# A feed-forward product with 20 small products for two halves of D, four chunks of F and three blocks of tokens, in place of Strassen's seven

## The chip, the cores and the metric

The kernel runs on one NeuronCore of a Trainium2 chip. TensorE (PE in the profile) multiplies matrices, VectorE (DVE) and ScalarE (ACT) work on SBUF and PSUM, GpSimd (POOL) works on SBUF alone, SyncE (SP) issues most of the DMAs. The metric is the device time of one execution in microseconds. The kernel before takes 1905.74 us, the median of three runs (1905.74 to 1906.42).

## The reference

```python
# x: (8, 3008, 256); w_in: (256, 2048); w_out: (2048, 256), all float32
X = np.fft.fft(np.fft.fft(x, axis=1), axis=2).real      # per batch: a 2-D DFT, real part
t = X.reshape(8 * 3008, 256)
h = t @ w_in
g = np.maximum(h, 0.0) ** 2
out = g @ w_out                                         # (24064, 256)
```

## The kernel before, in words

**Fronts.** For a batch b the DFT over the sequence is made as two tables, Pt and Qt (128 rows by NKT = 1505 frequencies), and one row that every partition needs, Et (spread over 128 partitions). The DFT over D is folded into w_in once, as G1, G2 and the column gE. Frequencies k and S-k share their work: with hP = G1'Pt and hQ = G2'Qt, the hidden rows are hP + gE Et + hQ for k and hP + gE Et - hQ for the mirrored frequency. The frequencies go in blocks of CK = 256 (the last has 225); a block is n columns of k and n of the mirrored ones, so 2n tokens. For each block a loop runs over NJ = 8 steps j; a step handles the chunks j and j + 8 of the 16 chunks of 128 of F. `front` (L887) does the four products of a step (L896) into two PSUM banks, hP and hQ, each 2 chunks by n; VectorE makes t = hP + gE Et (L900, twice) and then g = t + hQ (L903) and t - hQ reversed (L904). `relu` (L909) and `square` (L912) run in place on ScalarE. A front bank comes free when VectorE has read it; there are two such banks (pool psh), so the front of the next step may start when L900 has read hP, and its second half when L904 has read hQ.

**Sums and back.** `combine` (L914) makes the four sums of Strassen's scheme on GpSimd (L919 to L922, 256 wide each). `back` (L926) runs LAG = 2 steps later: seven products of n columns (L950), summed over j in four banks mA, mB, mC, mD (pool psm) for two halves of D by two sides of tokens. The weights' sums are in wsum (3 by 8 by 128). `gather` (L953) runs once a block, after j = 7: two copies on ScalarE (L981, L982), three sums on VectorE (L983 to L985), four on GpSimd (L986 to L989), into the tile c. `store` (L992) transposes c in 32 x 32 blocks on VectorE (L1021, L1023) and SP writes it out (L1027, L1029), two and three steps after the gather. The first block of batch 0 uses plain products instead (L935), because the weights' sums do not exist yet.

**Side work.** While batch b runs its 48 steps, the tables of batch b + 1 are made beside it, as a list of pieces with a cost in planner's units (`ahead`, L1031): folds of the input by symmetry on VectorE (`fold` L484, lines L500 to L530; `once` and `twice`, L553 to L605), and at the end of the list eight groups of small products: `even_n` (L655) and `odd_n` (L783), four products each on a tile of the pool psd (two banks), then joins on VectorE (L689 to L695, L777 to L797). `between` (L1193) takes pieces from the list inside `front`, on both sides of L903/L904; a table SHARE by j says how much of the units each step takes, and `pace` is all units over all shares. A piece of VectorE thus stands in VectorE's queue ahead of the next front's L900. The list for batch 1 also holds the rows of Et for all later batches, `dft_ops(None)`, stored to e_dram (L838). The last batch has no side work.

**Queues.** SP carries, in program order, the loads of x (each waits for the fold that frees its buffer), the stores (each waits for its transposes) and `load_e` (L861), one broadcast of Et for a batch at the end of its pieces. The start of the kernel (rounding of the weights, first DFT, first 10 steps) follows an order written out as a list of tokens (L1213).

What a step emits, in the main loop:

```python
g = front(b, k0, n, j, between)
...
back(at[2], at[3], g_, s_, final)      # the step two before
...
relu(n, g); square(n, g); combine(n, g)
```

Of the kernel before, what the change touches and what calls it, by code (L numbers as in the profile page):

```python
# [15 lines left out]
P = 128  # L16
R = 32
# [57 lines left out]
def table_places(S):  # L75

    places, at = [], 0
    for c, *_ in class_tiles(S):
        places.append(at)
        at += column_counts(S)[0][c]  # L80
    return places, at
# [3 lines left out]
def kernel(  # L85
# [22 lines left out]
    CK = 256  # L108
# [4 lines left out]
    PLACE, WT = table_places(S)  # L113
# [10 lines left out]
    sp = ctx.enter_context(tc.tile_pool(name="sp", bufs=3))  # L124
# [63 lines left out]
    cosT = const.tile([P, 2, WT], F32, name="cosT")  # L188
    sinT = const.tile([P, 2, WT], F32, name="sinT")
    wout = const.tile([P, NJ, 2, 2, H], F32, name="wout")  # L190
    wsum = const.tile([P, 3, NJ, H], F32, name="wsum")
# [5 lines left out]
    def load_table(tab, src, tiles, queue=nc.sync):  # L197

        for t in tiles:
            c, r0, step, rows = TILES[t]  # L200
            for i, (s0, count) in enumerate(row_tiles(S)):
                mine = [r for r in range(count) if (s0 + r - r0) % step == 0 and 0 <= (s0 + r - r0) // step < rows]
                if mine:
                    o, m = (s0 + mine[0] - r0) // step, len(mine)
                    while m % 15 and m % 16 and o + m < P and mine[0] + step * m < P:
                        m += 1
                    nk = NC[0][c]
                    queue.dma_start(out=tab[o:o + m, :, PLACE[t]:PLACE[t] + nk],
                                    in_=src[mine[0]:mine[0] + step * (m - 1) + 1:step, :, i, 0:nk])

    def turn_table(t):
# [3 lines left out]
        for kp in range(2):  # L215
            nk = NC[kp][c]
            nc.scalar.mul(sinT[0:rows, kp, at:at + nk], cosT[0:rows, kp, at:at + nk][:, ::-1], sind[0:rows, 0, P - 1:])
# [10 lines left out]
    assert 2 * NT <= 3 * NJ  # L228
# [33 lines left out]
    def scratch():  # L262

        return sp.tile([P, 4 * CK], F32, name="m", tag="s")[:, 0:2 * CH].rearrange("p (c e) -> p c e", c=2)
# [53 lines left out]
    def round_win(j, raw):  # L318

        def dst():  # L320
            win[j] = ep.tile([P, 2, CH], F32, name="win", tag="sB" if j % 2 else "sA")
# [29 lines left out]
    def sum_wout(js, half):  # L351

        b11, b12, b21, b22 = (wout[:, js, h, c] for c in range(2) for h in range(2))
        t2, t3, t4 = (wsum[:, i, js] for i in range(3))
        if half == 0:
            tt(out=t3, in0=b22, in1=b12, op=ALU.subtract)
            tt(out=b12, in0=b12, in1=b11, op=ALU.subtract)
        else:
            tt(out=t2, in0=b22, in1=b12, op=ALU.subtract)
            tt(out=t4, in0=t2, in1=b21, op=ALU.subtract)  # L360


    folded, from_psum, alone = {}, set(), set()
# [7 lines left out]
    def take_turn():  # L371
        for i, t, kp, k in ((BY_AC, ODD0, 1, 0), (BY_TWO, TWO, 1, 0), (BY_AB, ODD0, 0, 1)):
            for a, tab in enumerate((cosT, sinT, sinT)):
                r = slice(0, ROWS2)
                nc.scalar.mul(turn[r, a, i:i + 1], tab[r, kp, PLACE[t] + k:PLACE[t] + k + 1], -1.0 if a == 2 else 1.0)
# [8 lines left out]
    def part_table(tab, t):  # L384
# [4 lines left out]
        v = tab[0:rows, 0, at:at + nk]  # L389
# [10 lines left out]
    def columns(tab, t, part):  # L400
# [3 lines left out]
        return tab[:, 0, at + part * nq:at + (nk if part else nq)]  # L404

    def quarters(tab, part):
# [3 lines left out]
        return tab[0:HALF2, 0, at + part * n4:at + (n2 if part else n4)]  # L410
# [5 lines left out]
    e_dram = dp.tile([B, NKT], F32, name="e_dram")  # L416
    nc.gpsimd.memset(xe, 0.0)

# [202 lines left out]
    def dft_ops(b):  # L621
# [3 lines left out]
        def start():  # L625
            PQE[b] = [pq.tile([P, -(-NKT // 16) * 16], F32, name=nm, tag=nm)[:, 0:NKT] for nm in ("Pt", "Qt", "Et")]

        def group(kp, which):
# [6 lines left out]
            def product(ps, c, lone_e=False, only=None):  # L635

                ts = [t for t in range(NT) if TILES[t][0] == c]
                for t in ts if only is None else ts[only:only + 1]:
# [5 lines left out]
                    else:  # L644
# [3 lines left out]
                                     (cosT if lone_e else tab)[0:rows, kp, PLACE[t]:PLACE[t] + NC[kp][c]],  # L648
# [6 lines left out]
            def even_n():  # L655
                st["ps"] = psd.tile([P, 512], F32, name="pd", tag="d")[0:n]
# [126 lines left out]
            def odd_n():  # L783
                ps = psd.tile([P, 512], F32, name="pd", tag="d")[0:n]
# [21 lines left out]
            def join_1(only=None):  # L806
                dst = PQE[1][2][0:n] if b is None else PQE[b][which]
# [14 lines left out]
            ops = [(0.0, even_n), (0.5, join_4), (0.7, join_2), (0.0, odd_n), (1.1, join_1)]  # L822
            from_psum.update((join_4, join_2, join_turned))
            alone.update((even_n, odd_n))
            join_once, join_half = (lambda: join_odd("odd", n0)), (lambda: join_odd("half", n1))
            from_psum.update((join_once, join_half))
            if b != 0:
                ops.insert(4, (0.7, join_once) if kp else (0.5, join_turned))
            if kp:
                ops.insert(2, (0.5, join_half))  # L830
            return ops
# [5 lines left out]
        if b is None:  # L837
            ops.append((0.0, lambda: nc.sync.dma_start(out=e_dram[1:, :], in_=PQE[1][2][0:NE])))  # L838
        return ops

    def spread_e():

        _, qt, et = PQE[0]
        ps = psd.tile([P, CH], F32, name="pe", tag="d")[:, 0:CK]
        nc.tensor.matmul(ps, last.to_broadcast([P, P]), qt[:, 0:CK], start=True, stop=True)
        return lambda: nc.scalar.copy(et[:, 0:CK], ps)
# [3 lines left out]
    def spread_lower():  # L850
        _, qt, et = PQE[0]
        nc.gpsimd.dma_start(out=e_dram[0:1, CK:KH], in_=qt[P - 1:P, CK:KH])
        nc.gpsimd.dma_start(out=et[:, CK:KH], in_=e_dram[0:1, CK:KH].to_broadcast([P, KH - CK]))

    def store_upper():
        nc.sync.dma_start(out=e_dram[0:1, KH:], in_=PQE[0][1][P - 1:P, KH:])

    def load_upper():
        nc.sync.dma_start(out=PQE[0][2][:, KH:], in_=e_dram[0:1, KH:].to_broadcast([P, NKT - KH]))

    def load_e(b):  # L861
        nc.sync.dma_start(out=PQE[b][2], in_=e_dram[b:b + 1].to_broadcast([P, NKT]))


    def front_half(b, k0, n, j, h):

        pt, qt, _ = PQE[b]
# [7 lines left out]
    def new_g():  # L875
        return gp.tile([P, 2, 2, CK], F32, name="g", tag="g")

    def split_half(b, k0, n, j, h, g, ps):
        fc = j + NJ * h
        hP, hQ = ps[:, 0, 0:n], ps[:, 1, 0:n]  # L880
        t = hp.tile([P, 2, CK], F32, name="he", tag="he", bufs=1)[:, h, 0:n]
        nc.vector.scalar_tensor_tensor(out=t, in0=PQE[b][2][:, k0:k0 + n], scalar=gE[:, fc:fc + 1], in1=hP,
                                       op0=ALU.mult, op1=ALU.add)
        tt(out=g[:, h, 0, 0:n], in0=t, in1=hQ, op=ALU.add)
        tt(out=g[:, h, 1, 0:n][:, ::-1], in0=t, in1=hQ, op=ALU.subtract)

    def front(b, k0, n, j, between):  # L887

        pt, qt, et = PQE[b]
        ks, rows = slice(k0, k0 + n), P if b else P - 1  # L890
        g = new_g()
        pp, pq_ = (psh.tile([P, 2, CH], F32, name=nm, tag="h") for nm in ("hP", "hQ"))
        for to, w, v in ((pp, G1, pt), (pq_, G2[0:rows], qt[0:rows])):
# [3 lines left out]
        t = hp.tile([P, 2, CK], F32, name="he", tag="he", bufs=1)  # L897
        for h in range(2):
            fc = j + NJ * h
            nc.vector.scalar_tensor_tensor(out=t[:, h, 0:n], in0=et[:, ks], scalar=gE[:, fc:fc + 1],  # L900
                                           in1=pp[:, h, 0:n], op0=ALU.mult, op1=ALU.add)
        between(0)
        tt(out=g[:, :, 0, 0:n], in0=t[:, :, 0:n], in1=pq_[:, :, 0:n], op=ALU.add)  # L903
        tt(out=g[:, :, 1, 0:n][:, :, ::-1], in0=t[:, :, 0:n], in1=pq_[:, :, 0:n], op=ALU.subtract)  # L904
        between(1)
        return g

    def relu(n, g):
        act(g[:, :, :, 0:n], g[:, :, :, 0:n], AF.Relu)  # L909

    def square(n, g):
        act(g[:, :, :, 0:n], g[:, :, :, 0:n], AF.Square)  # L912

    def combine(n, g):  # L914
        s = sp.tile([P, 4, CK], F32, name="s", tag="s")
        g11, g12, g21, g22 = g[:, 0, 0, 0:n], g[:, 1, 0, 0:n], g[:, 0, 1, 0:n], g[:, 1, 1, 0:n]
        s1, s2, s3, s4 = (s[:, i, 0:n] for i in range(4))
        gt = nc.gpsimd.tensor_tensor
        return s, [lambda: gt(out=s1, in0=g21, in1=g22, op=ALU.add),  # L919
                   lambda: gt(out=s2, in0=s1, in1=g11, op=ALU.subtract),  # L920
                   lambda: gt(out=s3, in0=g11, in1=g21, op=ALU.subtract),  # L921
                   lambda: gt(out=s4, in0=g12, in1=s2, op=ALU.subtract)]  # L922

    acc = {}

    def back(n, j, g, s, final):  # L926

        if j == 0:
            for nm in ("mA", "mB") if s is None else ("mA", "mB", "mC", "mD"):
                acc[nm] = psm.tile([P, 2, CH], F32, name=nm, tag=nm)  # L930
        if s is None:
            for c in range(2):
                for h in range(2):
                    for side, nm in enumerate(("mA", "mB")):
                        nc.tensor.matmul(acc[nm][:, h, 0:n], wout[:, j, h, c], g[:, c, side, 0:n],  # L935
                                         start=j == c == h == 0, stop=j == NJ - 1 and c == 1, skip_group_check=True)
            return
        products = [("mA", 0, wout[:, j, 0, 0], g[:, 0, 0]),
                    ("mA", 1, wout[:, j, 0, 1], g[:, 1, 0]),
                    ("mB", 0, wsum[:, 2, j], g[:, 1, 1]),  # L940
                    ("mB", 1, wout[:, j, 1, 0], s[:, 0]),
                    ("mC", 0, wsum[:, 0, j], s[:, 1]),
                    ("mC", 1, wsum[:, 1, j], s[:, 2]),
                    ("mD", 0, wout[:, j, 1, 1], s[:, 3])]
        if final:
            banks = ("mA", 0), ("mC", 1), ("mC", 0), ("mB", 1), ("mA", 1), ("mB", 0), ("mD", 0)
# [465 lines left out]
```

## Time and profile before

The profiled execution took 1905.84 us; its span, from the first to the last instruction, is 1904.0 us. The granted clock of TensorE was 0.999 over it.

| what | value |
|---|---|
| PE busy | 1894.2 us (99%), 9216 instructions |
| DVE busy | 1371.9 us (72%), 2782 |
| ACT busy | 965.4 us (51%), 1227 |
| POOL busy | 1216.3 us (64%), 1732 |
| DMA, mean | 36 GB/s |
| batch to batch (same instruction of the transforms) | 230.5 us |
| step without side work (256 columns) | 4.75 us |
| last batch, 1700 to 1890 us | DVE 98.25 of 190 us busy |
| batch with side work, 800 to 1035 us | DVE 174.8, POOL 153.8 of 235 us busy |

How to read it: PE is busy in the whole span, so an instruction that takes longer on another engine costs time only if PE comes to wait for it. In the timeline, xN says how many instructions a row merges; the second number is the time from the first start to the last end. [...] The bracket at the end of a row is the idle time of that engine just before, and what ended it.

### The profile page before, as it was taken

To read this page: it belongs to the slowest core of one execution; us is meant where nothing else is said; L and a number is where in the kernel's file an instruction comes from. 1 tells how busy PE (TensorE), PEld (TensorE's weight loads), DVE (VectorE), ACT (ScalarE), POOL (GpSimd) and SP (SyncE) were. 2 spreads that over 40 slices of the span, in tenths; PEclk is the share of its full clock that TensorE was granted. 3 is DMA by queue.
4 is the path that set the end of the run, shared out by engine and by line. 5 is a ranking of instruction groups with operands and counts; after the bars stand their busy time and mean duration, and the time that the engine had idled before them with its cause. 6 is when DMAs were issued, how large, how long until landed. Compare 5 with 4: busy or idle time off the path is not lost.

```text
span 1904.0 us, 27430 instructions
## 1 busy us (share of the span) xinstructions
PE 1894.2 (99%) x9216; PEld 1700.6 (89%) x9216; DVE 1371.9 (72%) x2782; ACT 965.4 (51%) x1227; POOL 1216.3 (64%) x1732
## 2 busy tenths in 40 slices
PE   9999999999999999999999999999999999999998
PEld 7888898888988889888998889988899888998888
DVE  8688877776678766877677776787767777655554
ACT  5855555454454554445444554445544555444444
POOL 3376666766676666666666666666656666567665
PEclk9999999999999999999999999999999999999999
DMA  6431211120112101111011100211111101100101
GB/s 197 118 46 26 51 28 35 28 48 12 36 27 48 29 12 37 33 42 29 12 41 42 37 20 12 54 37 28 21 18 47 37 12 23 28 11 12 22 12 22
DMA packets 141077, 68.02 MB, mean 36 GB/s; under 512 B 125931, under 2 KB 131610, under 8 KB 140937
## 3 DMA queue, kind: packets, MB, share of 16 engines
q1 hardware_dynamic: 140374, 65.48, 15.3%
q8 instruction: 74, 1.21, 0.3%
q0 software_dynamic: 448, 0.69, 0.1%
q14 instruction: 67, 0.54, 0.1%
q10 hardware_dynamic: 114, 0.10, 0.0%
HBM read 41.54 MB, written 24.69 MB: 35 GB/s over the span
## 4 chain that ended last, share of the span: by engine, by line
PE 98%; DVE 1%; ACT 0%; DMA 0%; issue 0%; POOL 0%; DVEq 0%; ACTq 0%; POOLq 0%
PE mA L950 17%; PE mC L950 17%; PE mB L950 17%; PE hQ L896 16%; PE hP L896 16%; PE mD L950 8%; PE pd L647 1%; PE pd L765 1%; PE pg L334 1%; PE mA L935 1%; PE mB L935 1%; PE pd L739 1%; PE ph L870 0%; PE ph L872 0%; DMA xt<-in_x_dram 0%
## 5 line engine op out<-in xcount | busy, mean ns | idle before, releaser
L909 ACT ACTIVATE g<-g 128x1024 f32<-128x1024 f32 (+1 forms) x384 | 399.5, 1040 | 667.1 <-DVE g L904 614.6
L919 POOL TENSOR_TENSOR s<-g 128x256 f32<-128x256 f32 (+1 forms) x376 | 269.4, 717 | 559.3 <-ACT g L912 470.0
L900 DVE SCALAR_TENSOR_TENSOR he<-Et,gE,hP 128x256 f32<-128x256 f32 (+1 forms) x748 | 321.5, 471 | 346.6 <-PE hP L896 342.9
L912 ACT ACTIVATE g<-g 128x1024 f32<-128x1024 f32 (+1 forms) x384 | 399.5, 1041 | 12.0
L950 PE MATMUL mA<-g,wout 128*128 128x256 f32 (+1 forms) x1488 | 378.0, 376 | 0.0
L896 PE MATMUL hQ<-Qt,G 128*128 128x256 f32 (+3 forms) x1496 | 377.4, 375 | 0.4 <-DVE g L904 0.4
L896 PE MATMUL hP<-Pt,G 128*128 128x256 f32 (+1 forms) x1496 | 377.3, 375 | 0.0
L950 PE MATMUL mC<-s,wsum 128*128 128x256 f32 (+1 forms) x1472 | 372.0, 375 | 0.0
L896 PEld LDWEIGHTS hQ<-Qt,G 128*128 128x128 f32 (+1 forms) x1496 | 284.1, 190 | 32.8 <-PE hP L896 0.7
L896 PEld LDWEIGHTS hP<-Pt,G 128*128 128x128 f32 x1496 | 284.2, 190 | 32.2
L950 PEld LDWEIGHTS mC<-s,wsum 128*128 128x128 f32 x1472 | 279.7, 190 | 32.2
L950 PEld LDWEIGHTS mA<-g,wout 128*128 128x128 f32 x1488 | 278.9, 190 | 31.6 <-issue 0.3
L920 POOL TENSOR_TENSOR s<-s,g 128x256 f32<-128x256 f32 (+1 forms) x376 | 269.9, 718 | 29.5
L903 DVE TENSOR_TENSOR g<-he,hQ 128x512 f32<-128x512 f32 (+1 forms) x374 | 252.8, 676 | 45.8 <-DVE he L900 13.7
L922 POOL TENSOR_TENSOR s<-g,s 128x256 f32<-128x256 f32 (+1 forms) x376 | 276.9, 736 | 0.0
L921 POOL TENSOR_TENSOR s<-g 128x256 f32<-128x256 f32 (+1 forms) x376 | 272.7, 725 | 0.0
L904 DVE TENSOR_TENSOR g<-he,hQ 128x512 f32<-128x512 f32 (+1 forms) x374 | 250.5, 670 | 0.0
L950 PE MATMUL mB<-s,wout 128*128 128x256 f32 (+1 forms) x752 | 220.3, 375 | 0.0
L950 PE MATMUL mD<-s,wout 128*128 128x256 f32 (+1 forms) x752 | 220.3, 375 | 0.0
L950 PE MATMUL mB<-g,wsum 128*128 128x256 f32 (+1 forms) x736 | 216.0, 375 | 0.0
L950 PEld LDWEIGHTS mD<-s,wout 128*128 128x128 f32 x752 | 142.9, 190 | 16.1
L950 PEld LDWEIGHTS mB<-s,wout 128*128 128x128 f32 x752 | 142.9, 190 | 16.1
(207 smaller groups left out, 1515.4 us busy)
## 6 DMA issues: line engine op xcount, KB each, us to landing
out_dram<-os SPq DMA_DIRECT2D x288, 64.0 KB
xt<-in_x_dram SPq DMA_DIRECT2D x39, 384.0 KB
xt<-in_x_dram SPq DMA_DIRECT2D x63, 128.0 KB
Et<-e_dram SPq DMA_DIRECT2D x7, 752.5 KB
out_dram<-os SPq DMA_DIRECT2D x88, 56.0 KB
raw<-in_moe_w_in_dram SPq DMA_DIRECT2D x16, 256.0 KB
raw<-in_moe_w_out_dram SPq DMA_DIRECT2D x16, 256.0 KB
xt<-in_x_dram SPq DMA_DIRECT2D x2, 512.0 KB
```

What stands on the lines that cost most here:

```text
L896: nc.tensor.matmul(to[:, h, 0:n], w[:, fs], v[:, ks], start=h == 0, stop=True, skip_group_check=True)
L900: nc.vector.scalar_tensor_tensor(out=t[:, h, 0:n], in0=et[:, ks], scalar=gE[:, fc:fc + 1], in1=pp[:, h, 0:n], op0=ALU.mult, op1=ALU.add)
L903: tt(out=g[:, :, 0, 0:n], in0=t[:, :, 0:n], in1=pq_[:, :, 0:n], op=ALU.add)
L904: tt(out=g[:, :, 1, 0:n][:, :, ::-1], in0=t[:, :, 0:n], in1=pq_[:, :, 0:n], op=ALU.subtract)
L909: act(g[:, :, :, 0:n], g[:, :, :, 0:n], AF.Relu)
L912: act(g[:, :, :, 0:n], g[:, :, :, 0:n], AF.Square)
L919: return s, [lambda: gt(out=s1, in0=g21, in1=g22, op=ALU.add), lambda: gt(out=s2, in0=s1, in1=g11, op=ALU.subtract), lambda: gt(out=s3, in ...
L920: lambda: gt(out=s2, in0=s1, in1=g11, op=ALU.subtract),
L921: lambda: gt(out=s3, in0=g11, in1=g21, op=ALU.subtract),
L922: lambda: gt(out=s4, in0=g12, in1=s2, op=ALU.subtract)]
L935: nc.tensor.matmul(acc[nm][:, h, 0:n], wout[:, j, h, c], g[:, c, side, 0:n], start=j == c == h == 0, stop=j == NJ - 1 and c == 1, skip_gro ...
L950: nc.tensor.matmul(acc[nm][:, i, 0:n], w, v[:, 0:n], start=j == 0 and i == 0, stop=j == NJ - 1, skip_group_check=True)
```

## The change

The product with w_out is regrouped. Two steps (an even and an odd j) form a group: four chunks of 128 of F. The 2n tokens of a block are cut into three blocks of 2n/3 (n is 252, the last 246, so 168 and 164), and D stays in two halves. A scheme of 20 products does this 2 x 4 x 3 block product (24 when done plainly): 12 of them in `first_half` and 8 in `second_half`, each 168 columns wide. Per group of two steps the back has 20 products of 168 columns, where it had 14 of 256. NKT grows by one padding column to 1506 for this.

- **Banks.** The accumulators are six banks: F0, F1, F2 (for the first half) and S0 in pool psm, S1 and S2 in the two banks of pool psd. The transforms `even_n` and `odd_n`, which had psd, now take a bank of psh, the fronts' pool of two.
- **Order.** At step i the group (i - 3) // 2 runs: its first half at odd i, its second half at even i. A piece with transform products is no longer taken inside `front`: it runs from a hook after three products of the back (`pieces_beside(True)`), at most one a step, and its joins are part of the same piece (`even`, `odd`). Other pieces come after the front's four VectorE operations (`pieces_beside(False)`). SHARE is new.
- **Sums.** GpSimd makes 3 sums for an even step (`sums_even`: one of 336 columns, two of 168) and 8 for an odd one (`sums_odd`: four of 336, four of 168).
- **Gather.** Five parts: `early` (ScalarE copies F1 and two thirds of F2), `upper`, `lower` (with a ScalarE copy of two thirds of S0), `joins`, `rest`; 15 VectorE operations a block and none on GpSimd. They are emitted over four steps: early after the first half (j = 1 of the next block), upper and lower a step later, joins and rest in the two steps after that. The stores come at j = 5 and 6.
- **Weights.** 16 sums of weights (12 go to wsum, 4 overwrite w_out's chunks) on VectorE, in steps 8 to 14.
- **Et.** The whole-batch tile goes; each block loads its own window of n columns from e_dram by a broadcast on SP (`load_window`), six steps before the block starts, into a pool of two.
- Two tables of the first DFT have some of their columns moved into the buffers of the sums (LATE), to make room.

The core of the diff:

```diff
-    CK = 256
+    CK = 252
+    TB = 2 * CK // 3
...
             def even_n():
-                st["ps"] = psd.tile([P, 512], F32, name="pd", tag="d")[0:n]
+                st["ps"] = psh.tile([P, 512], F32, name="pd", tag="h")[0:n]
...
             def odd_n():
-                ps = psd.tile([P, 512], F32, name="pd", tag="d")[0:n]
+                ps = psh.tile([P, 512], F32, name="pd", tag="h")[0:n]
...
+    def sums_even(n, g):
+        ...
+        a0, a1, a2 = thirds(g, n)
+        gt(out=s[:, 0:2], in0=a0, in1=a2, op=ADD)
+        gt(out=s[:, 9], in0=a1[:, 0], in1=a2[:, 0], op=SUB)
+        gt(out=s[:, 10], in0=s[:, 9], in1=a1[:, 1], op=SUB)
+    def sums_odd(n, g, g_even, s):
+        ...
+        gt(out=s[:, 11], in0=b2[:, 0], in1=b1[:, 0], op=SUB)
+        gt(out=s[:, 2:4], in0=b0, in1=s[:, 0:2], op=ADD)
+        gt(out=s[:, 4:6], in0=b0, in1=a0, op=ADD)
+        gt(out=s[:, 4:6], in0=s[:, 4:6], in1=s[:, 10:11].to_broadcast([P, 2, tb]), op=SUB)
+        gt(out=s[:, 6], in0=b1[:, 0], in1=b1[:, 1], op=ADD)
+        gt(out=s[:, 7], in0=b2[:, 0], in1=s[:, 6], op=SUB)
+        gt(out=s[:, 6:9:2], in0=s[:, 2:4], in1=s[:, 6:8], op=ADD)
+        gt(out=s[:, 8], in0=s[:, 8], in1=b2[:, 1], op=ADD)
...
+    BANKS = {"F0": (psm, "mC"), "F1": (psm, "mD"), "F2": (psm, "mA"), "S0": (psm, "mB"), "S1": (psd, "d"), "S2": (psd, "d")}
...
+    def first_half(q, n, gA, gB, s, hook=None):
+        ...
+        run((("F0", 2, 0, r2[2]), ("F0", 1, 1, r2[1]), ("F0", 1, 2, s[:, 9]), ("F0", 0, (1, 2), r2[0]),
+             ("F0", 0, 3, s[:, 0]), ("F1", 2, (1, 1), r1[2]), ("F2", 1, (0, 0), r0[0]), ("F2", 1, 9, s[:, 1]),
+             ("F2", 0, (0, 3), r3[2]), ("F1", 0, 6, r0[2]), ("F1", 1, 5, r3[1]), ("F1", 1, 4, s[:, 11])), q, n, hook)
+    def second_half(q, n, s, hook=None):
+        ...
+        run((("S0", 0, 8, s[:, 2]), ("S0", 1, (0, 1), s[:, 4]), ("S0", 2, (0, 2), s[:, 8]), ("S1", 0, (1, 0), s[:, 6]),
+             ("S1", 1, 11, s[:, 10]), ("S1", 2, 10, s[:, 3]), ("S2", 0, 7, s[:, 7]), ("S2", 1, (1, 3), s[:, 5])),
+            q, n, hook)
...
+        def early():
+            nc.scalar.copy(cf[:, 2:5], F1)
+            nc.scalar.copy(cf[:, 0:2], F2[:, 0:2])
+        def upper():
+            tt(out=o1[0], in0=F0[:, 0], in1=u4, op=SUB)
+            tt(out=pair(1, 1), in0=F0[:, 1:3], in1=cf[:, 4:5].to_broadcast([P, 2, tb]), op=ADD)
+        def lower():
+            nc.scalar.copy(cs, S0[:, 0:2])
+            tt(out=o1[0], in0=o1[0], in1=S0[:, 0], op=SUB)
+            tt(out=o1[2], in0=o1[2], in1=S0[:, 2], op=ADD)
+            tt(out=cf[:, 3], in0=cf[:, 3], in1=S0[:, 1], op=SUB)
+            tt(out=vt[:, 0:2], in0=S1[:, 0:2], in1=cs, op=ADD)
+            tt(out=vt[:, 3:5], in0=S2[:, 0:2], in1=vt[:, 0:2], op=ADD)
+            tt(out=vt[:, 2], in0=S1[:, 2], in1=vt[:, 4], op=ADD)
+        def joins():
+            tt(out=vt[:, 5:7], in0=cf[:, 0:3:2], in1=vt[:, 2:4], op=ADD)
+            tt(out=o0[2], in0=vt[:, 6], in1=vt[:, 5], op=SUB)
+            tt(out=o0[2], in0=o0[2], in1=S0[:, 2], op=ADD)
+            tt(out=pair(0, 0), in0=cf[:, 1:4:2], in1=vt[:, 5:7], op=ADD)
+        def rest():
+            tt(out=pair(1, 1), in0=pair(1, 1), in1=vt[:, 0:4:3], op=ADD)
+            tt(out=pair(1, 1), in0=pair(1, 1), in1=vt[:, 1:3], op=SUB)
+            tt(out=o1[0], in0=o1[0], in1=vt[:, 4], op=ADD)
...
-    SHARE = (1.2, 0.0, 0.0, 0.7, 0.7, 1.0, 1.0, 1.0)
+    SHARE = (1.2, 1.2, 0.6, 0.0, 0.6, 0.8, 0.8, 1.2)
...
+    def pieces_beside(at_hook):
+        ...
+        while side:
+            t, f = side[0]
+            if f in beside:
+                if at_hook and spent + t / 2 <= 0:
+                    side.pop(0)
+                    f()
+                    spent += t
+                return
+            if t and (at_hook or t > room or spent + t / 2 > 0):
+                return
...
+            if j == 2 and i + NJ < len(steps):
+                load_window(*steps[i - 2 + NJ][:3])
+            made["g", i] = g = front(b, k0, n, j)
...
+            pieces_beside(False)
+            hook = (3, lambda: pieces_beside(True))
```

## The prediction

> **What bounds the kernel now.** I read the page first: the busy times and the chain that ended last.
>
> ```profile
> PE 1894.2 (99%) x9216; PEld 1700.6 (89%) x9216; DVE 1371.9 (72%) x2782; ACT 965.4 (51%) x1227; POOL 1216.3 (64%) x1732
> PE 98%; DVE 1%; ACT 0%; DMA 0%; issue 0%; POOL 0%; DVEq 0%; ACTq 0%; POOLq 0%
> ```
>
> TensorE never pauses: the waits charged to PE sum to about 5 us, all at the start. So a saving in matmul columns is worth its full length, as long as the other engines keep up. The timeline of a step without side work gives PE's pace and the slack of the others.
>
> ```profile
> 1701.05 1.03 PE L896 MATMUL hP<-Pt,G 128*128 128x256 f32 x4
> 1702.02 0.73 POOL L919 TENSOR_TENSOR s<-g 128x256 f32<-128x256 f32 x1 [1.84 <-ACT g L912]
> 1702.11 0.87 DVE L900 SCALAR_TENSOR_TENSOR he<-Et,gE,hP 128x256 f32<-128x256 f32 x2 [2.43 <-PE hP L896]
> 1702.82 0.73 POOL L920 TENSOR_TENSOR s<-s,g 128x256 f32<-128x256 f32 x1
> 1703.51 0.73 POOL L921 TENSOR_TENSOR s<-g 128x256 f32<-128x256 f32 x1
> ...
> 1705.80 1.03 PE L896 MATMUL hP<-Pt,G 128*128 128x256 f32 x4
> ```
>
> hP to hP is 4.75 us for 11 products. Each fp32 product is two passes, so 22 passes of 0.216 us. The start of the timeline gives other widths:
>
> ```profile
> 17.44 1.44 PE L647 MATMUL pd<-cosT,w 96*128 96x189 f32 x8
> 18.73 1.44 PE L647 MATMUL pd<-cosT,wsum 96*128 96x189 f32 x8
> ...
> 21.28 1.02 PE L647 MATMUL pd<-sinT,w 95*127 95x95 f32 x8
> 22.13 1.46 PE L647 MATMUL pd<-cosT,wsum 128*128 128x377 f32 x4
> ...
> 24.07 2.70 PE L647 MATMUL pd<-cosT,w 128*128 128x377 f32 x8
> 26.61 1.43 PE L647 MATMUL pd<-cosT,wsum 128*128 128x377 f32 x4
> ```
>
> By start to start a pass takes 0.106 us at 95 columns, 0.161 at 189, 0.3175 at 377. Last, the timeline of batch 3 (DVE with POOL), for what a VectorE operation with two SBUF operands costs:
>
> ```profile
> 801.09 0.73 POOL L921 TENSOR_TENSOR s<-g 128x256 f32<-128x256 f32 x1
> 801.18 1.79 DVE L530 TENSOR_TENSOR w<-sc 95x257 f32<-95x257 f32 x2
> 801.78 0.92 POOL L922 TENSOR_TENSOR s<-g,s 128x256 f32<-128x256 f32 x1
> ...
> 820.20 1.13 DVE L504 TENSOR_TENSOR fd<-xt 96x512 f32<-96x512 f32 x1
> ...
> 840.31 0.68 DVE L504 TENSOR_TENSOR fd<-xt 96x512 f32<-96x512 f32 x1
> 841.71 0.87 DVE L900 SCALAR_TENSOR_TENSOR he<-Et,gE,hP 128x256 f32<-128x256 f32 x2
> ```
>
> The same L504 takes 0.68 us or 1.13, and L530 about 0.9 instead of its median 0.417. The long ones begin while POOL runs. Counting all such fold operations from 331 to 1700 us: of 414, 168 (41%) began beside a POOL operation and took 0.43 us longer on average. L900, L903, L904 read PSUM and show no such split (477, 687, 681 ns throughout).
>
> **Products.** The line between 189 and 377 columns is 0.835 ns a column and 2.7 ns a pass: 0.143 us at 168, 0.213 at 252. The 95-column row shows that weight loads allow 0.106, so 168 stays a streaming time. Two steps then cost 16 x 0.213 + 40 x 0.143 = 9.13 us, a block of 252 36.5, the last (246) 35.6. A batch is 5 x 36.5 + 35.6 + 8 transforms x 0.89 (251.09) = 225.3, against a period of 230.5 (688.84 to 919.37): -5.2, times 8 = -41 after 0.7 us for the wider plain products of the first block. Straight proportion to 256 columns (0.1418) gives -53. Taken: **-47**.
>
> **POOL.** Four sums of 256 a step (728 to 745 ns) become, per two steps, six of 168 and five of 336. Issue intervals are 0.685 us at 256 and 0.625 at 225; the line through them gives 0.515 and 0.84, plus about 0.12 for each of five that read the sum just before (0.80 against 0.69 above). That is 7.9 us of 9.13, 86%; in the stretch 331 to 1690 us it is 68% now. POOL still keeps up, and its results come a step before the products that read them; but it leaves little quiet time. The 4 gather sums of a block leave POOL.
>
> **VectorE.** The gather (1.2 us: L983 to L985) becomes 15 operations. By L689/L695 with a PSUM operand (376 wide every 0.455 us, about 0.42 for 336; 0.245 for 168; 0.11 more where one reads the one before) and 0.44 and 0.25 for the six with SBUF operands alone, POOL quiet, they take 5.5. Per block of 8 steps, POOL quiet: fronts 8 x 2.15 (2.18 from 841.71 to 843.89 at 256 columns) = 17.2; stores 1.6; gather 5.5; folds. The folds of a batch took 182/5.9 = 30.8 us without their waits, shuffles 2.2: 33 for 37 units of the planner's costs. All pieces now sum to 48.6 units over 36.4 shares, 6.4 shares a block: 8.54 units, or 7.6 us. Sum 31.9 of PE's 36.5. Now the waits: 69 fold operations a batch make 16 a block, with the gather's six 22. Scaling 41% by POOL's share (0.86/0.68) gives 52%: 22 x 0.52 x 0.43 = 4.9 us. Walking the pairs (even steps' side work lies wholly beside the odd sums, of the odd steps' only the first operation) gives 6.6. Taken: 5.8. Ends: 3.9 (41% as now) and 9.5 (every one).
> So VectorE needs **37.7 us where PE needs 36.5**, in the blocks that fold. There PE loses 1.2 us, and I add 0.4 for order: the lower part of the gather sits at a step of 8 products (4.0 us of PE, about 6.5 of VectorE), the next front's L900 queues behind it some 2 us late, and S0 is read by the joins until about the moment at which the next second half wants it. With two front banks PE may run no further ahead than one front. Folds last 37/8.54 = 4.33 blocks of a batch: 4.33 x 1.6 = 6.9.
>
> [...]
>
> **Transforms in the fronts' banks.** The hook runs them after three products; even_n or odd_n must wait until L900 has read hP. On time that is at 1.9 us of the step, the hook at 2.6: free. After a gather VectorE is about 1 us late; then PE waits about 0.4, the nine or five products and the next front queue behind it, and the next hQ waits for the joins, about 0.9 more. Some one of eight pieces a batch meets this: 1.3. If none does 0, if all do 10. In these blocks VectorE has slack (0.89 us more PE per piece).
>
> **Moves at nothing.** ACT copies five and two 168-wide slices a block for two of 512: 1.4 us for 1.17, at 51% busy; the S0 copy now stands before a relu and delays relu, square and POOL's even sums by about 1 us, which are needed two steps later. Window loads (48 of 126 KB for 7 Et loads of 752) join SP's queue six steps (27 us) before use; POOL's one broadcast landed in 3.9. SP waits up to 33.9 us on the stores' transposes, but those come after the load in program order. POOL loses one of its two e_dram issues (0.6). If a window were late, the first L900 of 48 blocks would wait.
>
> **Ends.** The 32 weight sums of 256 columns replace 8 of 512 (7.6 us by L356 to L360): about 15, over seven steps rather than four: +3, 0 to +5. After the last product stand 4 more dependent VectorE operations and a POOL chain of 6 us before it: +3, 1 to 6.
>
> **Sum.** The profiled execution took 1905.84 (span 1904.0 and 1.84 around it), 0.1 from the median. Seven batches carry side work for the next: 7 x (6.9 + 1.3) = 58. 1905.8 - 47 + 58 + 6 = 1922.8, given as **1923**.
>
> **Rivals.**
> PE's saving lands (faster): if VectorE meets POOL no oftener than now, 3.9 us of waits make 35.8 of 36.5; only the 0.4 and 1.3 stay, 7 x 3.0 = 21: 1905.8 - 47 + 21 + 6 = **1886**, and about 1865 with no stall. It decides at 4.9 us of waits: VectorE below 36.8 leaves at most 0.7 a block. For it: 41% at 68% POOL shows that order protects the folds. Against it: POOL's quiet time falls from 1.84 us a step to about 1.2 in two. Chance 0.36.
> VectorE bound as forecast, 1910 to 1960: 0.45.
> Contention worse: a POOL operation between two fold operations also grows (0.92 at 801.78), POOL fills, 85% meet it for 0.45: 8.4 us, VectorE 40.3, 4.2 x 4.33 + 1.3 = 19.5 a batch, 136: **2001**. For it: two of two in a row wait at 801.18. Against: stalls thin POOL's share again. Chance 0.13.
> Gains and stalls cancel, within 0.2% (3.8 us, about what a measurement of this kernel can tell from none): 0.06.
>
> From these: faster 0.36, same 0.06, slower 0.58. The forecast's own range is 1910 to 1960; 1870 to 1975 leaves out about 2 in 10: the no-stall end and most of the worse contention.
>
> **What would show it.** A pass of 168 at 0.142 to 0.143; the last batch, which has no side work, shorter by 5 to 6 us; blocks that fold at 37 to 39 us, with PE idle at the start of a step or of a second half, ended by VectorE (the sums into g, the gather's joins); fold operations with a mean near 0.6 for 257 columns (0.528 now); POOL 80% or more. Wrong if PE stays at 98%: then the time is near 1880; wrong in size if the 257-wide folds average 0.8.

## The result and the profile after

The changed kernel takes 1998.43 us (1996.1 to 1999.31) where the kernel before takes 1905.74: a ratio of 1.0484, 95% interval 1.0465 to 1.0502. The forecast was 1923, with 1975 as the upper end. Its profiled execution took 1996.1 us, span 1994.3.

The page of the changed kernel, its busy times, the granted clock by slices (50 us each) and the first line of the chain that ended last:

```profile
PE 1899.8 (95%) x11408; PEld 1765.2 (89%) x11408; DVE 1722.7 (86%) x3462; ACT 966.6 (48%) x1274; POOL 1564.0 (78%) x2111
PEclk9998999999999999999999999999999999999999
PE 14%; DVE 4%; ACT 0%; POOL 0%; issue 0%; DVEq 0%; POOLq 0%; ACTq 0%
```

PE was at 99% and is at 95%: 94.5 us of the span are now idle (9.8 before), while its busy time did not fall (the same instructions are busy for 1857.0 us in e6, an experiment below). VectorE stands in the chain with 4% where it had 1%; the chain breaks off after 18% of the span, so its shares are not comparable beyond that. In the fourth slice the clock is below 9 tenths. The view of the waits says what PE waits for. Columns: engine, the instruction that waited and what ended the wait, then us in total, times, longest.

```profile
PE F L990 <- DVE c L1050: 17.7, 12, 2.7
PE hQ L928 <- DVE dc L717: 13.4, 6, 2.2
PE hQ L928 <- DVE Pt L717: 10.5, 6, 2.1
PE hQ L928 <- DVE g L935: 9.5, 28, 0.4
PE pd L669 <- DVE he L932: 8.0, 3, 3.8
PE hP L928 <- DVE he L932: 6.7, 5, 2.2
```

All of them are ended by VectorE: by `upper` of the gather (L1050, it frees F0), by the joins of the transforms (L717, they free a front bank), by the fronts' own sums (L932, L935). POOL's sums end 1.1 us of them.

The timeline of the last batch, where nothing runs beside its steps, shows the new pace (second number: us of the merged row; x6 is three products of two passes each):

```profile
1805.17 0.45 PE L990 MATMUL S<-s,wsum 128*128 128x168 f32 x2
1805.45 1.02 PE L990 MATMUL S<-s,wout 128*128 128x168 f32 x6
...
1806.31 1.02 PE L990 MATMUL S<-s,wsum 128*128 128x168 f32 x6
1807.16 0.45 PE L990 MATMUL S<-s,wout 128*128 128x168 f32 x2
1807.45 1.01 PE L928 MATMUL hP<-Pt,G 128*128 128x252 f32 x4
```

Six passes of 168 from 1806.31 to 1807.16 are 0.142 us each. A block of this batch takes 36.40 us (37.99 before): the saving is there, and where nothing competes it lands in full.

Where the 90.3 us of span went, from the starts of the steps (first hP of each) in both traces:

| stretch | before, us | after, us | difference | forecast |
|---|---|---|---|---|
| start to step 10 | 97.3 | 94.8 | -2.5 | +3 |
| batch 0, steps 10 to 47 | 188.0 | 227.0 | **+39.0** | +2.3 |
| batches 1 to 6 | 6 x 230.53 | 6 x 239.4 | **+53.2** | +14.0 |
| batch 7, to its last front | 219.2 | 212.5 | -6.65 | -5.9 |
| tail | 16.3 | 23.6 | +7.3 | +3 |

The forecast column is the prediction's sum by batches: -47/8 for the products, +8.2 for side work. Batch 0 and batches 1 to 6 hold nearly all of the miss.

The windows of batch 0 (window, us; then busy us and instructions of PE, PEld, DVE, ACT, POOL; granted clock, DMA share, GB/s), before:

```profile
97.30:285.30 188.00, 187.50 (x933) 167.94 (x933) 157.50 (x336) 100.67 (x155) 121.61 (x168) 1.00 0.21 38
```

and after:

```profile
94.80:321.80 227.00, 198.98 (x1153) 180.28 (x1152) 201.38 (x419) 100.56 (x160) 155.95 (x210) 0.96 0.19 30
```

VectorE was busy for 157.5 of 188 us (84%) in batch 0 already before, where its mean over the whole span was 72%. After, it is busy for 201.4 us, more than the 188 that PE had needed. That batch's list is also the densest: it holds the rows of Et for all batches and has only the steps from 12 on to run in.

The timeline of batch 3 shows two ways in which VectorE makes PE wait. The first lines: `upper` (L1050) stands at the gather, the joins of a transform (the last is L717) behind it, and hQ waits 2.24 us for its bank. The last lines: `rest` (L1068 to L1070), ops with two SBUF operands, beside POOL; they take 2.7 us in a row, and the next joins (L799) wait behind them.

```profile
966.64 0.49 DVE L1050 TENSOR_TENSOR c<-F,cf 128x336 f32<-128x336 f32 x1
...
967.76 0.35 DVE L717 TENSOR_TENSOR dc<-db,pd 128x188 f32<-128x188 f32 x1
...
968.25 1.09 PE L928 MATMUL hQ<-Qt,G 128*128 128x252 f32 x4 [2.24 <-DVE dc L717]
...
976.25 0.97 DVE L1068 TENSOR_TENSOR c<-c,vt 128x336 f32<-128x336 f32 x1
...
976.93 1.05 POOL L968 TENSOR_TENSOR s<-s 128x336 f32<-128x336 f32 x1
977.25 1.09 DVE L1069 TENSOR_TENSOR c<-c,vt 128x336 f32<-128x336 f32 x1
...
978.27 0.67 DVE L1070 TENSOR_TENSOR c<-c,vt 128x168 f32<-128x168 f32 x1
...
978.86 0.25 DVE L799 TENSOR_TENSOR pd<-oc,pd 128x94 f32<-128x94 f32 x1
```

### The profile page after: what moved, and what is told of

It is laid out like the page before. It is cut to its first block, busy times and chain, and to the rows that moved or that the text cites. A ratio compares the mean times of both kernels' runs of the same rounds, so it can differ in the third digit from the quotient of the medians.

```text
span 1994.3 us, 33439 instructions
## 1 busy us (share of the span) xinstructions
PE 1899.8 (95%) x11408; PEld 1765.2 (89%) x11408; DVE 1722.7 (86%) x3462; ACT 966.6 (48%) x1274; POOL 1564.0 (78%) x2111
## 5 line engine op out<-in xcount | busy, mean ns | idle before, releaser
L939 ACT ACTIVATE g<-g 128x1008 f32<-128x1008 f32 (+1 forms) x384 | 399.8, 1041 | 684.6 <-DVE g L935 541.1
L932 DVE SCALAR_TENSOR_TENSOR he<-ew,gE,hP 128x252 f32<-128x252 f32 (+1 forms) x748 | 317.4, 464 | 150.9 <-PE hP L928 149.8
L928 PE MATMUL hQ<-Qt,G 128*128 128x252 f32 (+3 forms) x1496 | 385.3, 380 | 36.2 <-DVE dc L717 13.4
L942 ACT ACTIVATE g<-g 128x1008 f32<-128x1008 f32 (+1 forms) x384 | 399.4, 1040 | 12.0
L928 PE MATMUL hP<-Pt,G 128*128 128x252 f32 (+1 forms) x1496 | 379.3, 376 | 6.7 <-DVE he L932 6.7
L990 PE MATMUL F<-s,wsum 128*128 128x168 f32 (+1 forms) x1504 | 343.1, 310 | 0.0
L990 PE MATMUL F<-g,wout 128*128 128x168 f32 (+1 forms) x1504 | 314.5, 312 | 0.0
L990 PE MATMUL F<-g,wsum 128*128 128x168 f32 (+1 forms) x1504 | 280.8, 310 | 17.7 <-DVE c L1050 17.7
L934 DVE TENSOR_TENSOR g<-he,hQ 128x504 f32<-128x504 f32 (+1 forms) x374 | 253.4, 678 | 49.9 <-DVE he L932 4.4
L990 PE MATMUL S<-s,wout 128*128 128x168 f32 (+1 forms) x1504 | 282.3, 306 | 0.1
L990 PE MATMUL S<-s,wsum 128*128 128x168 f32 (+1 forms) x1504 | 277.0, 307 | 4.7 <-DVE c L1064 3.3
L935 DVE TENSOR_TENSOR g<-he,hQ 128x504 f32<-128x504 f32 (+1 forms) x374 | 250.5, 670 | 0.0
L968 POOL TENSOR_TENSOR s<-s 128x336 f32<-128x336 f32 (+1 forms) x188 | 184.0, 979 | 14.7
```

The costliest lines, as they stand in the source:

```text
L928: nc.tensor.matmul(to[:, h, 0:n], w[:, fs], v[:, ks], start=h == 0, stop=True, skip_group_check=True)
L932: nc.vector.scalar_tensor_tensor(out=t[:, h, 0:n], in0=window[b, k0][:, 0:n], scalar=gE[:, fc:fc + 1], in1=hP[:, h, 0:n], op0=ALU.mult, op ...
L934: tt(out=g[:, :, 0:n], in0=t[:, :, 0:n], in1=hQ[:, :, 0:n], op=ALU.add)
L935: tt(out=g[:, :, n:2 * n][:, :, ::-1], in0=t[:, :, 0:n], in1=hQ[:, :, 0:n], op=ALU.subtract)
L939: act(g[:, :, 0:2 * n], g[:, :, 0:2 * n], AF.Relu)
L942: act(g[:, :, 0:2 * n], g[:, :, 0:2 * n], AF.Square)
```

## The experiments

The theory from these views: POOL's sums, by reading SBUF for most of the time, lengthen VectorE's two-operand work until VectorE is the bound. The rivals: the order of the gather in VectorE's queue; the front bank that the transforms hold; POOL itself being late. Ratios are to the kernel before.

### Order: only the place of the wait moves

**e1_upper_first** puts the waiting parts of the gather ahead of the step's side pieces:

```diff
+        while pending and pending[0][0] <= i:
+            pending.pop(0)[1]()
         hook = None
         if PLAIN <= i < len(steps):
...
-        while pending and pending[0][0] <= i:
-            pending.pop(0)[1]()
```

> The changed kernel with the gather's parts (upper, joins, rest) emitted ahead of the side pieces of their step, so that they stand right behind the front's four VectorE operations. Theory (VectorE full because its fold operations wait for POOL; PE's waits are what is left over): the waits of the first F0 product for L1050 (17.7 us in all) go, and with them about half of the stretches at half clock (some 8 us); part comes back as later pieces. 1965 to 1985. Rival (the order in VectorE's queue at the gather is the whole cause): below 1940. Rival (the transforms in the fronts' banks are the cause): 1990 or more.

Measured: 2017.25 us, 1.0583 (1.0567 to 1.0598). The waits for `upper` are gone, but PE now waits 24.9 us (longest 4.2) for L717, 22.9 for L932 and 15.0 for L935. **e7_upper_alone** moves `upper` alone, and takes no transform at j = 2 and 4:

```diff
+        if pending and pending[0][0] <= i and pending[0][2:]:
+            pending.pop(0)[1]()
...
-            hook = (3, lambda: pieces_beside(True))
+            if i < per or j not in (2, 4):
+                hook = (3, lambda: pieces_beside(True))
```

> The changed kernel without transform pieces at j = 2 and 4 (from the second batch on), and with the gather's upper part alone ahead of the side pieces of its step; joins and rest stay behind them. If order is what makes the first F0 product wait, its 25.8 us and the stretches at half clock behind them go: 1945 to 1965. If VectorE is full and the wait only moves: 1975 to 1995.

Measured: 2000.75, 1.0498 (1.0482 to 1.0514): no wait for `upper`, and 38.3 us for L932 at L669. **e2_not_at_gather** has the second edit alone:

> The changed kernel with no transform piece at j = 2 and j = 4 (from the second batch on), where the gather's parts stand in VectorE's queue. Rival (front banks): the waits of hQ for the joins (dc L717 and Pt L717, 23.9 us) and most stretches at half clock go, 1955 to 1970. Theory (VectorE full): the pieces' work moves to other steps and is paid there in part, 1975 to 1990.

Measured: 1987.0, 1.0432 (1.041 to 1.0455). The waits for L717 are gone (23.9 us), yet only 11 us of time: those for `upper` rise from 17.7 to 25.8 us, those at L669 from 8.0 to 19.7. e1 and e7 came out above what the theory had expected, and e1 where the rival on the front banks had put it; e2 speaks against that rival, which had expected 1955 to 1970. Three orders, three lists of waits, and a loss of 81 to 111 us in each: what is short is VectorE's time more than its order.

### POOL's reads are the cause

**e3_quiet_pool** leaves the eleven sums of a pair of steps out; the products read a tile that is filled once.

```diff
-        gt(out=s[:, 0:2], in0=a0, in1=a2, op=ADD)
-        ...
+        if not fixed:
+            fixed.append(sp.tile([P, 12, TB], F32, name="s", tag="s"))
+            nc.gpsimd.memset(fixed[0], 0.5)
+        return fixed[0][:, :, 0:tb]
```

> The changed kernel with GpSimd's eleven sums of a pair left out: the products read a tile filled once, so the output is not the reference's. Every VectorE and PE instruction stays. Theory (fold and gather operations wait for POOL): L550 at 257 columns falls to about 0.42 us, VectorE to about 32 us a block that folds, and the time to 1865 to 1890. Rivals (banks, or order alone): the waits of PE stay, 1950 or more.

Measured: 1885.7, 0.9892 (0.9876 to 0.9909). A batch takes 226.6 us, a block with folds 36.2 to 36.6, with VectorE at 29.5 to 30.6. But here POOL neither reads, nor is busy, nor can it be late. **e6_pool_writes_only** keeps it busy: each sum becomes a memset of 840 or 504 columns.

```diff
-        gt(out=s[:, 0:2], in0=a0, in1=a2, op=ADD)
-        ...
+        write(s, 5, 0)
+        ...
+    def write(s, size, at):
+        nc.gpsimd.memset(s[:, at:at + size], 0.5)
```

> The changed kernel with each of the eleven sums replaced by a GpSimd memset of about the same length into the same part of the sums' tile (840 or 504 columns, some 0.8 and 0.5 us by the 1.586 us of a memset of 1792): GpSimd is as busy, the products still wait for it, but it reads nothing. The output is not the reference's. [...]

Measured: 1885.62, 0.9894 (0.9877 to 0.991), with POOL busy for 1342.9 us (71%): the loss is gone though POOL is busy and the products depend on it. The groups by form for the folds' 257-wide sums, before, after, and with POOL only writing (count; busy us, mean ns; idle before):

```profile
L530 DVE TENSOR_TENSOR w<-sc 96x257 f32<-96x257 f32 x84 | 41.1, 528 | 0.7
```

```profile
L550 DVE TENSOR_TENSOR w<-sc 96x257 f32<-96x257 f32 x84 | 62.3, 781 | 0.7
```

```profile
L550 DVE TENSOR_TENSOR w<-sc 96x257 f32<-96x257 f32 x84 | 31.7, 418 | 0.7
```

So 112.8 us of the changed kernel's time (1998.43 against 1885.62) hang on POOL's reads. In e6 317 of 654 VectorE operations with two SBUF operands begin beside a memset and none of them is longer; VectorE is busy for 1477.7 us there and for 1477.3 in e3, without the memsets.

Two kernels let only a part of POOL read. **e11_even_sums_read** has the three sums of even steps as they are and memsets for the eight of odd steps; **e12_odd_sums_read** the reverse, with three memsets in `sums_even`. The edit of e11, in `sums_odd`:

```diff
-        gt(out=s[:, 11], in0=b2[:, 0], in1=b1[:, 0], op=SUB)
-        ...
+        for size, at in ((3, 9), (5, 2), (5, 4), (5, 4), (3, 6), (3, 7), (5, 6), (3, 8)):
+            write(s, size, at)
```

> The changed kernel with POOL's three sums of an even step as they are and the eight of an odd step replaced by memsets of the same tiles (so the output is not the reference's). POOL reads for about 2.1 of 9.1 us. Threshold theory: VectorE's waits grow to some 2 us a block, 32.5 of 36.4, and TensorE hardly waits: 1886 to 1896. Proportional theory: 112.8 us of difference (1998.4 against 1885.6 with no reads) times 0.27: about 1916.

> The mirror case: the eight sums of an odd step as they are, the three of an even step replaced by memsets (so the output is not the reference's). POOL reads for about 5.8 of 9.1 us. Threshold theory: VectorE near 36 of 36.4 us in the folding blocks: 1915 to 1945. Proportional theory: 1885.6 and 0.73 of 112.8: about 1968.

Measured: 1890.44, 0.9917 (0.9902 to 0.9932), and 1967.88, 1.0324 (1.0309 to 1.034). Neither theory has both: e11 comes out as the threshold had it, e12 as the proportion had it. The traces tell why. Against the lengths in e3, VectorE's `tensor_tensor` operations without a PSUM operand (for the gather: all of its own) are longer, after 331 us, by the sums in this table. The 60 folds that are `scalar_tensor_tensor` are not in it; they add 6.8 us before and 16.1 after.

| kernel | folds and joins: begun beside POOL | longer by, us | gather: longer by, us | time, us |
|---|---|---|---|---|
| before | 162 of 402 (40%) | 69.5 | | 1905.7 |
| after | 367 of 415 (88%) | 150.3 | 53.6 | 1998.4 |
| e11, even sums | 343 of 405 | 13.0 | 0 | 1890.4 |
| e12, odd sums | 369 of 413 | 115.8 | 50.3 | 1967.9 |
| e8, no joins | 365 of 413 | 162.1 | left out | 1919.7 |
| e10, before and one sum | 326 of 403 (81%) | 134.8 | | 1910.1 |

What counts is what POOL does when the folds run. In the changed kernel 242 of the 367 meetings are with odd sums, and they make 111 of the 150 us; the gather's are 126 of 160. In batch 0, e11 takes 196.4 us and e12 222.4.

**e8_no_joins** takes seven VectorE operations from each gather (`joins` and `rest`, six of them with SBUF operands alone) and copies three slices on ScalarE instead:

```diff
-            tt(out=vt[:, 5:7], in0=cf[:, 0:3:2], in1=vt[:, 2:4], op=ADD)
-            ...
+            for k in range(3):
+                nc.scalar.copy(o0[k], vt[:, k])
```

> The changed kernel with the gather's last two parts, joins and rest (seven VectorE operations a block, six of them with SBUF operands alone), left out; three ScalarE copies fill one half of c, so the output is not the reference's. VectorE loses about 4.5 us of 37 to 38 a block that folds and falls below PE's 36.4. If the gather's added load is what pushes VectorE over, 1915 to 1945; if the folds' waits alone are the cause, 1965 or more.

Measured: 1919.73, 1.0072 (1.0057 to 1.0087), a batch 228.5 us. The folds wait as much as in the changed kernel (162 us), but in three of batch 3's four blocks with folds it costs nothing: they take 36.2 to 36.6 us, with VectorE at 32.3 to 34.5. In the fourth, 37.9 us with VectorE at 34.7, PE idles for 1.3. Batch 0 still takes 216.1.

### One part alone, on the kernel before

**e10_one_more_sum** adds one unused sum of 256 columns per step to POOL, **e5_busy_pool** two:

```diff
+                   lambda: [gt(out=idle[:, 0:n], in0=g11, in1=g21, op=ALU.add) for k in range(1)]]
```

> The kernel before with one more sum of 256 columns on POOL a step (its result is not used), POOL at 76 to 80% in place of 64%. Theory: the two-operand folds meet POOL more often, 60 to 75% of them in place of 41%, and grow, but VectorE keeps room in a block of 38 us; POOL keeps up; no change of more than 1%: 1905 to 1920. Rival (POOL late, as with two more sums): TensorE waits for sums by more than 5 us together: 1925 to 1950.

> The kernel before, and GpSimd given two more sums of 256 columns in each step (written to a tile that nobody reads): about 4.1 of 4.75 us busy, as in the changed kernel. The contention by itself, without the new gather and without the new banks. Theory (only the sum of the loads passes PE): fold operations at 257 columns go from 0.53 to about 0.8 us, VectorE from 30 to about 34 of 38 us in a block that folds, and PE hardly waits: 1905 to 1920. Rival (contention alone makes PE wait): 1940 or more.

e10: 1910.12, 1.0022 (1.0012 to 1.0031), POOL at 81%. The folds' meetings double (40 to 81%) and batches 1 to 6 still take 230.53 us each, to the hundredth; all of the 4 us lies in batch 0 (188.0 to 192.1). e5: 1975.29, 1.0364 (1.0349 to 1.038), with POOL at 92% and PE waiting for its sums:

```profile
PE mB L953 <- POOL s L921: 8.4, 12, 0.8
PE mC L953 <- POOL s L923: 7.5, 25, 0.4
```

The forecast for e5 failed by this. It is another case, POOL late, and says nothing on the changed kernel, where such waits are 1.1 us in all.

**e4_front_banks_alone** gives the kernel before the transforms in a front bank, from a hook after three products, with the joins in the same piece:

```diff
-                st["ps"] = psd.tile([P, 512], F32, name="pd", tag="d")[0:n]
+                st["ps"] = psh.tile([P, 512], F32, name="pd", tag="h")[0:n]
...
+            return [(1.5 if kp else 1.1, even), (1.7 if kp else 1.5, odd)]
...
+            if k == 3 and hook:
+                hook()
```

> The kernel before with one part of the change: the transforms take a bank of the fronts' pool, run after three of the seven back products, and make their joins at once; Strassen's seven products, POOL's sums and the shares stay. Theory: where VectorE has slack (30 of 38 us) the bank costs nearly nothing, 1904 to 1912. Rival (the bank itself costs): 60 pieces by 0.5 to 1 us, 1935 to 1965.

Measured: 1929.17, 1.0123 (1.0108 to 1.0138): 23 us for what the prediction gave 9 in all, and what the expectation had at nearly nothing. Batches 1 to 6 take 233.1 to 234.8, the excess in the block with the first transforms:

```profile
PE hQ L903 <- DVE dc L695: 14.9, 7, 2.3
```

### The clock after a wait

In the changed kernel the granted clock falls to one half eleven times before its end, for 41 us together; before, only in its last 2 us. **e9_waits_by_dose** makes waits of rising length in the kernel with quiet POOL:

```diff
             pieces_beside(False)
+            if i >= per and j == 5 and BLOCKS[1][0] <= k0 <= BLOCKS[4][0] and b < B - 1:
+                for k in range(12 + 4 * (b - 1) + k0 // CK - 1):
+                    nc.vector.memset(idle, 0.5)
```

> The kernel with quiet POOL (the sums left out, its output is not the reference's) and, in 24 steps of batches 1 to 6 (j = 5 of blocks 1 to 4), 12, 13, ... 35 VectorE memsets behind the front's four operations: a rising delay of the next front, about 0.2 us a memset. Theory: a wait of TensorE above some length, near 2 us, is followed by one stretch of 3.41 us at half the granted clock, so the larger doses show both and the time is 1905 to 1935; the shorter waits show none. Rival: the half clock comes from something else than the wait (the load, POOL), and the granted clock stays full here up to the end: 1900 to 1920, as much longer than 1885.7 as the waits are together.

Measured: 2090.94 us in one execution. The size was missed, since a memset takes 0.38 us from start to start, not 0.2; the waits rise from 1.55 to 10.4 us. The timelines of the first two doses:

```profile
358.49 1.12 PE L928 MATMUL hP<-Pt,G 128*128 128x252 f32 x4 [1.55 <-DVE he L932]
359.98 1.09 PE L928 MATMUL hQ<-Qt,G 128*128 128x252 f32 x4 [0.37 <-DVE g L935]
...
398.08 1.12 PE L928 MATMUL hP<-Pt,G 128*128 128x252 f32 x4 [2.32 <-DVE he L932]
399.58 2.02 PE L928 MATMUL hQ<-Qt,G 128*128 128x252 f32 x4 [0.37 <-DVE g L935]
```

The wait of 1.55 us costs its length. After that of 2.32 the clock is at one half from 399.17 to 402.58, and hQ's four passes take 2.02 us in place of 1.09. All 23 waits from 1.91 us up are followed by half clock: one stretch of 3.41 us up to waits of 3.5, one or two to 4.2, two to 6.2, two or three to 7.3, then three, four at 10.4. The rival (load or POOL) falls, since POOL is idle here.

But the length of a wait is not all. In the changed kernel 22 waits between 90 and 1900 us last 1.9 us or more, and only 11 of them are followed by half clock. Within each trace all these stretches start on one grid of 3.413 us: in the changed kernel the one at 981.00 starts 243 such windows after the one at 151.56. There every stretch follows a window of the grid in which PE idled 1.98 us or more, and no window with 1.79 or less is followed by one. e4 shows it best, with a wait of 2.25 us in each of six batches:

```profile
468.02 1.79 PE L903 MATMUL hQ<-Qt,G 128*128 128x256 f32 x4 [2.25 <-DVE dc L695]
469.61 1.91 PE L959 MATMUL mA<-g,wout 128*128 128x256 f32 x4
...
937.52 1.10 PE L903 MATMUL hQ<-Qt,G 128*128 128x256 f32 x4 [2.25 <-DVE dc L695]
938.46 1.03 PE L959 MATMUL mA<-g,wout 128*128 128x256 f32 x4
```

The wait that ends at 468.02 lies within one window (464.88 to 468.29), and half clock follows; so it is in three more batches. The wait that ends at 937.52 is cut by a window's end at 935.92, where the grid puts it, into 0.65 and 1.60 us, and the clock stays full; so it is in one more batch (0.46 and 1.79). These two batches take 233.1 us, the other four 234.7 to 234.8. The limit is not exact: in e2 and e5 some stretches follow windows with 1.4 to 1.7 us of idle PE.

## Why the prediction was wrong

The step that failed is the price of the side work, "7 x (6.9 + 1.3) = 58". Against e6, where POOL doesn't read, the changed kernel loses 33.4 us in batch 0 and 12.8 in each of batches 1 to 6, 110 in all.

**Right: products.** A pass of 168 takes 0.142, the last batch is 6.65 us shorter (forecast 5 to 6), and with POOL silent the kernel takes 1885.7: the forecast's rival "PE's saving lands" had 1886. That this fits to 0.3 us is partly luck: in e3 batch 0 takes 5.6 us more than before, and batches 1 to 6 take 3.9 less each, where the rival had seven alike.

**Right: POOL.** Its operations sum to 85% of the stretch 331 to 1690 (forecast 86%; 68% before by the same count), and PE waits 1.1 us for its sums.

**Right in sum, wrong in its parts: VectorE in a folding block.** Batch 3's four such blocks take 36.6, 39.9, 38.5 and 37.7 us, mean 38.2; the forecast was 36.5 + 1.6 = 38.1. Over batches 1 to 6 these blocks lose 7.5 us a batch against e6, where 6.9 was forecast. But the share of folds beside POOL, scaled with POOL's busy share from 41% to 52%, is 88%. The 40% of before was no rate: the folds sat in POOL's gaps, and e10 shows them lose that at once, to 81%. Two things hid it: the gather's operations meet POOL less (62%), and the work without waits is 30.2 (the mean of the four blocks in e6), not 31.9. In these blocks of batches 1 to 6 the waits come to 6.8 us a block (5.6 for the folds, 1.2 for the gather) against 5.8, so that VectorE needs 37.0 us where 37.7 was forecast. The 257-wide mean of 781 ns against "near 0.6" shows it.

**Wrong: "Seven batches carry side work for the next: 7 x (6.9 + 1.3)".** Batch 0 is not one of seven alike. The windows of before gave VectorE 84% there against 74% in the next batch, and the prediction took VectorE's load per block from batches 1 to 6 alone. In e6 the window of batch 0 is

```profile
94.90:288.60 193.70, 186.83 (x1154) 173.50 (x1153) 167.22 (x419) 101.46 (x160) 130.33 (x208) 1.00 0.21 35
```

With the longer operations VectorE's work, 167.2 us there, is 201.4, above PE's 186.8, so VectorE has more to do than PE. Batch 0 makes +36.7 of the miss of 75 us: 33.4 from the reads, and 3.3 that e6 has too (26 of the 32 weight sums, 10.9 us of VectorE in e6, also fall into it). Of the 33.4, 21.2 are more idle time of PE and 12.2 longer busy time, of which half clock (17.1 us in this batch) can make at most 8.5. e10 says the same from the other side: batch 0 is the one that pays.

**Wrong: "Some one of eight pieces a batch meets this: 1.3".** A batch takes 239.4 us, 12.8 more than e6's 226.6; 7.5 of that are the folding blocks, 5.3 the two blocks with transforms. e6's own excess over a batch without stalls (224.6, an estimate from its blocks of 36.4 and the 0.89 a transform of the prediction) is 2.0. So the blocks with transforms lose 7.3 a batch, inside the bounds of 0 and 10 that were given for the bank; how much of it is the bank and how much the gather beside it was not separated. The step assumed that a piece is late only by VectorE's delay of 1 us; the joins stand whole behind `upper` or `rest` (2.24 and 2.1 us in the trace), and e4 shows 2.5 to 4.2 a batch even on the kernel before.

**Not priced: the clock.** The sum gives each wait its own length. Half of the changed kernel's waits of 1.9 us or more are followed by 3.41 us or more at half clock, and PE loses up to half of that time (in e9 hQ took 2.02 us there, 1.09 outside). 41 us at half clock make at most 20 us of the 90.

**Also off:** order. "S0 is read by the joins" was named as the stall; S0 (L1064) cost 3.3 us, F0 at `upper` 17.7, since `upper` stands behind the side pieces. The experiments on order show that this choice was worth little. The tail is +7.3, just past the 1 to 6 that was given; the weight sums cost nothing by step 10, and the rest of them run in batch 0.

The rival "contention worse" (2001) was given 0.13. No run shows its 0.45 us a meeting; the folds' meetings cost 0.43 before (69.5/162) and 0.41 after (150.3/367). Its share of meetings (85%, measured 88%) and its time (1998) fit, its place does not: it put 18 us a batch into folding blocks, where 7.5 were lost. What decided was that two places with little room on VectorE, batch 0 and the gather beside transforms, pay more than the mean.

**Open:** the change's parts were not separated to the end. The sum of e10 (+4.3) and e4 (+23.0) on the kernel before is far below 112.8. Neither holds the gather's 15 operations, and e8, without seven of them, is 78.7 us faster than the changed kernel; that the gather makes the difference is argued from this, not shown by itself. In batch 0 the clock's part is known only by the bound above.

## What to carry to other kernels

Read the load of the engine that is to become the second bound in every stage, the densest first: its mean over the span (here VectorE's 72%) says nothing of the stage that will pay (84% in batch 0). A share of meetings between two engines measured under one order isn't a rate that scales with load: here one more sum a step took it from 40 to 81% (e10), and the change to 88%. So price every meeting, and measure which of them cost: here those with POOL's reads did, 0.41 us each, and those with its memsets did not (e6). And a wait of TensorE of some 2 us can cost more than its length, as 11 of 22 did in the changed kernel: where it fell into one window of the grid, each 3.41 us at half clock behind it cost up to 1.7 us more, an estimate from the half clock.

## What the runs showed of the hardware

- **POOL's reads, not its work, hold VectorE up.** A fold of 257 columns takes 0.418 us on average where POOL only writes (e6) and 0.781 where it sums (after); a meeting costs about 0.41 us (150.3/367). POOL's own operations are longer too while the folds run: L968, 336 wide, means 1.001 us from 331 to 1690 us against 0.941 in the last batch (1772 to 1960), which has no folds; L956, 168 wide, 0.696 against 0.545.
- **The clock answered to single waits, by their place.** Stretches at half clock last 3.41 us or a multiple and start on one grid of 3.413 us in each trace. In the changed kernel each of the eleven follows a window of the grid with 1.98 us or more of idle PE; in e2 and e5 some follow windows with 1.4 to 1.7. The changed kernel's wait of 2.24 us that ended at 968.25 was cut by a window's end into 1.34 and 0.91 us and was followed by none; that of 2.10, ended at 980.59, lay within one window and was followed by half clock.
